# Raw weights of the last layer in an idle buffer, output weights split in the third cosine stage, the logits' maximum by TensorE

## The chip, the cores and the metric

The kernel runs on one core of a Trainium2 chip. The metric is the device time of one execution in microseconds (us); shown is the median of three runs. The profile is of one more execution, whose own time stands beside its span.

## The reference

Sliding-window attention with sinks gives 1536 tokens of 512 features. A mixture of eight experts follows, whose gates are normalised eight times over the rows and columns, and then one wide layer with a cosine.

```python
def _moe_ref(x, w_gate, w1, w2):
    N, D = x.shape                      # 1536, 512
    E = w_gate.shape[1]                 # 8
    logits = x @ w_gate
    logits = logits - logits.max()
    P = np.exp(logits)
    for _ in range(8):
        P /= P.sum(1, keepdims=True) + 1e-09
        P /= P.sum(0, keepdims=True) + 1e-09
        P *= N / E
    out = np.zeros((N, D), dtype=np.float32)
    for e in range(E):
        h = np.maximum(x @ w1[e], 0.0)  # w1[e]: 512 x 1024
        ye = h @ w2[e]                  # w2[e]: 1024 x 512
        out += P[:, e:e + 1] * ye
    return out

def _moe2_ref(x, w_in, w_out):          # 512 x 2048, 2048 x 512
    h = x @ w_in
    g = h * np.cos(h)
    return g @ w_out
```

## The kernel before

The tokens are two batches of 768 (b = 0, 1). After attention there are ten layers: e = 0 to 7 are the experts, with relu; e = 8 and 9 are the two halves of the wide layer, 1024 columns each, with the cosine. A layer does, for each batch in turn, a first product and a second product on TensorE. All operands of products are f32 numbers split into a high and a low f16 half, so that a product is three matmuls for each piece of depth.

The first product (L975 for the experts, in `g1_sums`, L992, for the cosine layers) uses seven products of sums of blocks in place of eight. It needs the x operand `XO[b]` and the first-layer operand `W1O`, both of which hold seven sums of blocks. It is 28 steps long (`GT`, a step is six matmuls of 128x384), the second product (L1043) 24 (`HT_`); a layer is thus 104 steps, and each step ends in `tick()`. The four pairs of cosine layer and batch are called here the first to fourth cosine stage; in them part of the second product is woven into the first as filler. The results of the first product go through five banks: ScalarE copies one (L1014), DVE adds others to it (L1006), and then the cosine runs as ScalarE L900, DVE L903, ScalarE L908 and L909, DVE L912, POOL L914 (high half of `hh`) and L916 (low half). In the expert layers the row is L943, L947, L890, L891, and POOL L892 for the low half.

Side work stands in the program at ticks. `put(t0, every, steps)` puts one step at tick t0 from now, the next `every` ticks later, and each engine runs its instructions in the order in which they were written. A split writes the high half on ScalarE (L190) and at the next tick the low half on DVE (L191).

- Weights of layer e + 1 are prepared in layer e. `w_load` brings the raw f32 ones by SP's queue into a stage buffer of 16 KB per partition (tag "st", one buffer), and finds their scale from the largest element (DVE L168), or, for the output weights of layer 9, from the sum of squares (ScalarE L171, which writes unneeded squares into part of `W2S[1]`). `w1_split` makes sums on POOL (L274 to L277) and splits all into `W1O`; `w2_split` splits eight blocks f = 0 to 7 into `W2S[e % 2]`. The second product of layer 8 reads `W2S[0]`, that of layer 9 `W2S[1]`.
- The x operands of the cosine layers are made from the experts' sum by `x_operand`, six for each batch: three sums into T (L205 to L207), splits of x and T into `xs`, and a transposing DMA on SP (L213) into `XO[b]`. Batch 0's belong to the end of layer 7, batch 1's to layer 8.
- `probabilities` finds the largest logit: DVE reduces each row, and a POOL all-reduce over the partitions gives the maximum, which ScalarE's exponential takes (L660).

The times of the last layer's weights in layer 8 are t2 (its output weights) and t1 (its input weights): tick of the loads, of the first scale step, its spacing, tick of the first split, its spacing.

Of the kernel before, what the change touches and what calls it, by code (L numbers as in the profile page):

```python
# [40 lines left out]
def kernel(  # L41
# [256 lines left out]
    def w2_split(e, st):  # L298
        def sp(f):
            w = W2S[e % 2]  # L300
            split(w[:, 0, f], w[:, 1, f], st["w2"][:, f], wsc[e, "w2"][0])

        return [lambda f=f: sp(f) for f in range(NF)]


    def attention():
# [344 lines left out]
        def probabilities():  # L651
            gm = sm.tile([128, 1], F32, tag="gm", name="gm")
            ga = sm.tile([128, 1], F32, tag="ga", name="ga")
            lf = LG.rearrange("p t e -> p (t e)")
            nc.vector.tensor_reduce(out=gm, in_=lf, axis=AX.X, op=ALU.max)
            nc.gpsimd.partition_all_reduce(ga, gm, 128, MAXOP)

            def rest():
                nc.vector.tensor_scalar(out=ga, in0=ga, scalar1=-1.0, scalar2=None, op0=ALU.mult)
                nc.scalar.activation(out=P.rearrange("p t e -> p (t e)"), in_=lf, func=AF.Exp, bias=ga)  # L660

            return rest

# [146 lines left out]
    def experts(before):  # L810
# [60 lines left out]
        def x2(b):  # L871
# [9 lines left out]
            def ops(c, i):  # L881
                put(2, 1, [x_operand(b, c, i, sx2[b][0])])

# [165 lines left out]
        def layers(e, b, act, so):  # L1049
# [24 lines left out]
            if e == E - 1:  # L1074
                amx, xops = x2(b)

                put(5, 4, [amx[t] for t in tiles])
                put(26, 1, amx[-1:])
                if b:

                    put(HT_ + 5, 7.0, xops[:3])
                    put(HT_ + GT + 9, 4.0, xops[3:])
                else:
                    put(HT_ + 5, 7.0, xops)
            late = None
# [78 lines left out]
        put(T0 + 0, 2, [lambda f=f: gate(f) for f in gates[1]])  # L1164
        put(T0 + 15, 1, [lambda: put(10, 1, [probabilities()])])
        for n, f in enumerate(sinkhorn()):
# [3 lines left out]
        for e in range(E + 2):  # L1170
# [6 lines left out]
            if e + 1 < E + 2:  # L1177

                junk = W2S[1][:, 0, 0:2].rearrange("p f w -> p (f w)").bitcast(BF16) if e == E else None
                ld2, ld1 = w_load(e + 1, "w2", None, st, junk), w_load(e + 1, "w1", None, st)  # L1180

# [6 lines left out]
                if e == E:  # L1188
                    t2, t1 = (0, 6, 5.0, 41, 1.4), (GT + HT_ + -1, GT + HT_ + 5, 3.0, GT + HT_ + GT + 10, 0.5)
                if e == E - 1:  # L1190
# [78 lines left out]
```

## Time and profile before

| what | value |
| --- | --- |
| time, median of 3 runs | 1347.63 us (1346.87 to 1348.05) |
| profiled execution, its own time | 1346.85 us |
| its span from first to last instruction | 1345.1 us |
| mean granted TensorE clock | 0.972 |
| TensorE matmul busy | 1271.7 us, 95% |
| VectorE (DVE) busy | 881.6 us, 66% |
| ScalarE (ACT) busy | 695.7 us, 52% |
| GpSimd (POOL) busy | 654.0 us, 49% |

An engine's share is an average over the whole span; what a step is worth shows only in the stretch where it lies. The line numbers of all rows are those of the kernel before.

### The profile page before, as it was taken

To read this page: it belongs to the slowest core of one execution; us is meant where nothing else is said; L and a number is where in the kernel's file an instruction comes from. 1 tells how busy PE (TensorE), PEld (TensorE's weight loads), DVE (VectorE), ACT (ScalarE), POOL (GpSimd) and SP (SyncE) were. 2 spreads that over 40 slices of the span, in tenths; PEclk is the share of its full clock that TensorE was granted. 3 is DMA by queue.
4 is the path that set the end of the run, shared out by engine and by line. 5 is a ranking of instruction groups with operands and counts; after the bars stand their busy time and mean duration, and the time that the engine had idled before them with its cause. 6 is when DMAs were issued, how large, how long until landed. Compare 5 with 4: busy or idle time off the path is not lost.

```text
span 1345.1 us, 19675 instructions
## 1 busy us (share of the span) xinstructions
PE 1271.7 (95%) x7267; PEld 677.3 (50%) x7267; DVE 881.6 (66%) x1747; ACT 695.7 (52%) x1414; POOL 654.0 (49%) x818
## 2 busy tenths in 40 slices
PE   5657899999999999999999999999999998999998
PEld 4533546454554545455454555545455544445454
DVE  7986734765557655754755585385566778787674
ACT  6665846372644437164453716335372657666452
POOL 5666672540633364173335427234541847377543
PEclk7858999999999999999999999999999998999999
DMA  9999662021113310501321150132112241400001
GB/s 242 178 166 211 138 113 76 2 70 63 57 63 96 108 64 30 174 1 63 102 102 63 32 173 1 63 113 92 63 36 87 44 103 28 104 1 1 32 17 48
DMA packets 138641, 108.25 MB, mean 80 GB/s; under 512 B 98096, under 2 KB 113456, under 8 KB 138544
## 3 DMA queue, kind: packets, MB, share of 16 engines
q1 hardware_dynamic: 124464, 76.69, 22.1%
q0 software_dynamic: 7168, 25.17, 5.9%
q10 hardware_dynamic: 6912, 5.13, 1.5%
q8 instruction: 57, 0.93, 0.3%
q14 instruction: 40, 0.33, 0.1%
HBM read 71.84 MB, written 11.53 MB: 62 GB/s over the span
## 4 chain that ended last, share of the span: by engine, by line
PE 69%; DVE 6%; POOL 4%; ACT 4%; issue 3%; DMA 1%; POOLq 0%; DVEq 0%; ACTq 0%
PE bank L1043 37%; PE bank L975 28%; PE bank L992 4%; DVE tmp L1006 2%; DMA xo<-xs 1%; POOL hh L892 1%; DVE tmp L912 1%; DVE tmp L903 1%; DVE w1o L191 1%; ACT xs L190 1%; DVE xs L191 0%; ACT tmp L908 0%; ACT tmp L900 0%; POOL S L274 0%; POOL S L276 0%
## 5 line engine op out<-in xcount | busy, mean ns | idle before, releaser
L1043 PE MATMUL bank<-w2s,hh 128*128 128x512 f16 x2880 | 637.9, 379 | 5.1 <-POOL hh L916 2.4
L975 PE MATMUL bank<-xo,w1o 128*128 128x384 f16 x2688 | 449.3, 327 | 12.6 <-ACT tmp L943 6.4
L1043 PEld LDWEIGHTS <-hh 128*128 128x128 f16 x2880 | 280.3, 98 | 338.9 <-POOL hh L916 6.3
L892 POOL TENSOR_TENSOR hh<-tmp,hh 128x384 f16<-128x384 f32 x256 | 232.8, 929 | 362.7 <-ACT tmp L891 360.9
L975 PEld LDWEIGHTS <-w1o 128*128 128x128 f16 x2688 | 260.6, 98 | 188.7 <-issue 18.3
L943 ACT ACTIVATE tmp<-bank 128x384 f32<-128x384 f32 x192 | 93.4, 487 | 341.0 <-PE bank L975 340.8
L947 DVE TENSOR_TENSOR tmp<-bank,tmp 128x384 f32<-128x384 f32 x192 | 104.1, 553 | 173.9 <-ACT tmp L943 127.7
L992 PE MATMUL bank<-xo,w1o 128*128 128x384 f16 x672 | 122.1, 333 | 7.3 <-ACT tmp L1014 3.6
L1112 DVE SCALAR_TENSOR_TENSOR acc<-bank,PS,acc 128x512 f32<-128x512 f32 x84 | 62.9, 748 | 82.4 <-PE bank L1043 81.8
L890 ACT ACTIVATE hh<-tmp 128x384 f16<-128x384 f32 x192 | 98.9, 515 | 10.7 <-DVE tmp L947 10.6
L891 ACT ACTIVATE tmp<-tmp 128x384 f32<-128x384 f32 x192 | 100.4, 523 | 6.1
L992 PEld LDWEIGHTS <-w1o 128*128 128x128 f16 x672 | 66.7, 99 | 60.1 <-issue 13.4
L914 POOL TENSOR_SCALAR hh<-tmp 128x384 f16<-128x384 f32 x64 | 45.8, 715 | 85.2 <-DVE tmp L912 72.9
L190 ACT ACTIVATE w1o<-S,s 128x1024 f16<-128x1024 f32 x40 | 45.8, 1145 | 74.5 <-POOL S L277 74.0
L168 DVE TENSOR_REDUCE wm<-st 128x1 f32<-128x1024 f32 x68 | 81.5, 1208 | 0.0
L191 DVE SCALAR_TENSOR_TENSOR w1o<-st,s,w1o 128x512 f16<-128x512 f32 x72 | 65.9, 948 | 13.5 <-ACT w1o L190 13.4
L916 POOL TENSOR_TENSOR hh<-tmp,hh 128x384 f16<-128x384 f32 x64 | 69.4, 1084 | 5.3
L191 DVE SCALAR_TENSOR_TENSOR w1o<-S,s,w1o 128x1024 f16<-128x1024 f32 x40 | 55.0, 1375 | 20.3 <-ACT w1o L190 20.3
L1006 DVE TENSOR_TENSOR tmp<-bank,tmp 128x384 f32<-128x384 f32 x112 | 59.1, 547 | 12.1 <-PE bank L992 8.1
L191 DVE SCALAR_TENSOR_TENSOR w2s<-st,s,w2s 128x512 f16<-128x512 f32 x72 | 56.4, 797 | 9.7 <-ACT w2s L190 9.5
L190 ACT ACTIVATE w2s<-st,s 128x512 f16<-128x512 f32 x72 | 46.6, 708 | 22.8 <-DVE s L160 22.8
L587 POOL TENSOR_TENSOR parts<-xo,parts 128x512 f16<-128x512 f32 (+1 forms) x38 | 42.9, 1128 | 27.3 <-ACT parts L581 16.4
(187 smaller groups left out, 1297.3 us busy)
## 6 DMA issues: line engine op xcount, KB each, us to landing
st<-in_moe_w_dram SPq DMA_DIRECT2D x56, 512.0 KB, 6.2
f<-in_moe_w_in_dram POOLq DMA_DIRECT2D x16, 512.0 KB, 4.4
f<-in_moe_w_out_dram POOLq DMA_DIRECT2D x16, 512.0 KB, 4.2
w2p<-in_moe_w_dram SPq DMA_DIRECT2D x8, 512.0 KB, 4.4
w_in<-x POOLq DMA_DIRECT2D x16, 256.0 KB, 4.8
w_out<-x POOLq DMA_DIRECT2D x16, 256.0 KB, 4.2
st<-w_out SPq DMA_DIRECT2D x8, 512.0 KB, 5.4
st<-w_in SPq DMA_DIRECT2D x8, 512.0 KB, 6.1
```

The lines of the kernel that those rows point to most:

```text
L168: nc.vector.tensor_reduce(out=dst, in_=src, axis=axis, op=ALU.max, apply_absolute_value=True)
L190: nc.scalar.activation(out=hi, in_=src, func=AF.Copy, scale=s)
L191: late.append(lambda: nc.vector.scalar_tensor_tensor(out=lo, in0=src, scalar=s, in1=hi, op0=ALU.mult, op1=ALU.subtract))
L890: nc.scalar.activation(out=hi, in_=src, func=AF.Relu)
L891: nc.scalar.activation(out=dst, in_=src, func=AF.Relu)
L892: nc.gpsimd.tensor_tensor(out=lo, in0=dst, in1=hi, op=ALU.subtract)
L943: nc.scalar.activation(out=t, in_=ps, func=AF.Copy)
L947: nc.vector.tensor_tensor(out=t, in0=ps, in1=t, op=ALU.add)
L975: nc.tensor.matmul(ps, W1O[:, j0 + c, wi, o, kk, :], XO[b][:, kk, o, xi, :], start=(n == 0 and o in (0, 5, 1)), stop=(n == 5), skip_group_ ...
L992: nc.tensor.matmul(ps, W1O[:, j, wi, o, kk, :], XO[b][:, kk, o, xi, :], start=(n == 0), stop=(n == 5))
L1006: nc.vector.tensor_tensor(out=t, in0=x, in1=y, op=ALU.add)
L1043: nc.tensor.matmul(ps, HH[:, hi, f, t * 128:(t + 1) * 128], w[:, wi, f, :], start=(f == order[0] and n == 0), stop=(f == order[-1] and n = ...
```

## The change

The logits' maximum is no longer found by POOL: DVE spreads the row maxima on a diagonal, TensorE multiplies that by ones so that every partition has all of them in a bank, and DVE takes the maximum.

The sums of the x operands are made by DVE for batch 0 and by POOL, as before, for batch 1. Batch 0's operands are put at ticks 57, 62, 67, 72, 77, 82 of layer 7 (they were at 57, 64, 71, 78, 85, 92), batch 1's at 5, 11, 17, 23, 29, 35 of layer 8 (5, 12, 19, 37, 41, 45).

The raw input weights of the last layer are loaded into `W2S[1]`, which is idle in layer 8, seen as f32, at tick 55 (51), and no longer into the stage buffer. The raw output weights stay in the stage buffer until they are split: their squares are at ticks 34, 38, 42, 46 (6, 11, 16, 21), their eight splits at 101, 103, 105, 107, 110, 112, 114, 117 (41 to 50). Layer 9 begins at tick 104. The splits go in the order f = 0, 4, 1, 5, 2, 6, 3, 7.

```diff
--- before.py
+++ after.py
@@ -300,7 +300,8 @@
             w = W2S[e % 2]
             split(w[:, 0, f], w[:, 1, f], st["w2"][:, f], wsc[e, "w2"][0])
 
-        return [lambda f=f: sp(f) for f in range(NF)]
+        fs = [f for j in range(NJ) for f in (j, NJ + j)] if e == w1.shape[0] + 1 else range(NF)
+        return [lambda f=f: sp(f) for f in fs]
 
 
     def attention():
@@ -652,14 +653,21 @@
             gm = sm.tile([128, 1], F32, tag="gm", name="gm")
             ga = sm.tile([128, 1], F32, tag="ga", name="ga")
             lf = LG.rearrange("p t e -> p (t e)")
+            spread = stage.tile([128, 512], F32, tag="x", name="gdiag", bufs=2)[:, 0:128]
             nc.vector.tensor_reduce(out=gm, in_=lf, axis=AX.X, op=ALU.max)
-            nc.gpsimd.partition_all_reduce(ga, gm, 128, MAXOP)
-
-            def rest():
+            nc.vector.tensor_scalar(out=spread, in0=eye, scalar1=gm, scalar2=None, op0=ALU.mult)
+            box = []
+
+            def product():
+                box.append(ring["x"].next()[:, 0:128])
+                nc.tensor.matmul(box[0], ones, spread, start=True, stop=True)
+
+            def read():
+                nc.vector.tensor_reduce(out=ga, in_=box[0], axis=AX.X, op=ALU.max)
                 nc.vector.tensor_scalar(out=ga, in0=ga, scalar1=-1.0, scalar2=None, op0=ALU.mult)
                 nc.scalar.activation(out=P.rearrange("p t e -> p (t e)"), in_=lf, func=AF.Exp, bias=ga)
 
-            return rest
+            return [product, read]
 
 
         at = defaultdict(list)
@@ -879,7 +887,7 @@
                 scales(m1, 1, 1e-30, res, f"x2{b}", lambda *s: sx2.__setitem__(b, s))
 
             def ops(c, i):
-                put(2, 1, [x_operand(b, c, i, sx2[b][0])])
+                put(2, 1, [x_operand(b, c, i, sx2[b][0], g=nc.gpsimd if b else nc.vector)])
 
             return ([lambda t=t: absmax(m[:, t:t + 1], a[:, t, :]) for t in range(NT)] + [scl],
                     [lambda c=c, i=i: ops(c, i) for c in range(2) for i in range(U3)])
@@ -1078,10 +1086,9 @@
                 put(26, 1, amx[-1:])
                 if b:
 
-                    put(HT_ + 5, 7.0, xops[:3])
-                    put(HT_ + GT + 9, 4.0, xops[3:])
+                    put(HT_ + 5, 6.0, xops)
                 else:
-                    put(HT_ + 5, 7.0, xops)
+                    put(HT_ + 5, 5.0, xops)
             late = None
             if e >= E:
                 for t in ps:
@@ -1162,7 +1169,7 @@
         put(6, 1, w1_rest[5:9])
         put(10, 1, w1_rest[9:])
         put(T0 + 0, 2, [lambda f=f: gate(f) for f in gates[1]])
-        put(T0 + 15, 1, [lambda: put(10, 1, [probabilities()])])
+        put(T0 + 15, 1, [lambda: put(3, 3, probabilities())])
         for n, f in enumerate(sinkhorn()):
             put(T0 + 29 + 3 * (n // 3) + (0, 2, 3)[n % 3], 1, [f])
         st = {}
@@ -1177,7 +1184,9 @@
             if e + 1 < E + 2:
 
                 junk = W2S[1][:, 0, 0:2].rearrange("p f w -> p (f w)").bitcast(BF16) if e == E else None
-                ld2, ld1 = w_load(e + 1, "w2", None, st, junk), w_load(e + 1, "w1", None, st)
+                raw = W2S[1].bitcast(F32).rearrange("p a b w -> p (a b) w") if e == E else None
+                raw = raw.rearrange("p (a b) w -> p a (b w)", b=2) if raw is not None else None
+                ld2, ld1 = w_load(e + 1, "w2", None, st, junk), w_load(e + 1, "w1", raw, st)
 
 
                 t2, t1 = (3, 9, 3.0, 28, 2.25), (GT + HT_ + -16, GT + HT_ + 6, 2.5, GT + HT_ + GT + 0, 1.0)
@@ -1186,7 +1195,7 @@
                 if e == 1:
                     t2, t1 = (GT + 1, GT + 9, 2, GT + 20, 1.2), (GT + 31, GT + 46, 2, GT + HT_ + GT + 4, 1.3)
                 if e == E:
-                    t2, t1 = (0, 6, 5.0, 41, 1.4), (GT + HT_ + -1, GT + HT_ + 5, 3.0, GT + HT_ + GT + 10, 0.5)
+                    t2, t1 = (0, 34, 4.0, GT + HT_ + GT + 21, 2.3), (GT + HT_ + 3, GT + HT_ + 9, 3.0, GT + HT_ + GT + 10, 0.5)
                 if e == E - 1:
                     t2, t1 = (3, 8, 2.5, 24, 1.25), (35, 43, 2.0, GT + HT_ + GT + 0, 1.0)
                 put(t2[0], 0, ld2[:4])
```

In the changed kernel the lines after the first hunk are numbered higher: L892 becomes L900, L900 L908, L908 L916, L909 L917, L1014 L1022, L1115 L1122.

On POOL, where the largest logit is found in layer 0 (`gm` and `ga` are its row maxima and the result, S the first-layer weights' sums), there stood:

```order
L185 TENSOR_TENSOR xs<-T,xs 128x4x128
L892 TENSOR_TENSOR hh<-tmp,hh 128x384 x8
L656 ISA
L656 ISA ga<-gm 128x1
L892 ISA
L892 TENSOR_TENSOR hh<-tmp,hh 128x384 x8
L274 TENSOR_TENSOR S<-st 128x256
```

and now stand:

```order
L207 TENSOR_TENSOR T<-acc_75,T 128x128
L185 TENSOR_TENSOR xs<-T,xs 128x4x128
L900 TENSOR_TENSOR hh<-tmp,hh 128x384 x16
L274 TENSOR_TENSOR S<-st 128x256
L275 TENSOR_TENSOR S<-S,st 128x256
```

The all-reduce and two instructions without operands beside it are gone, and the sixteen subtractions follow one another.

On ScalarE, near the end of the first cosine stage (L171 is a sum of squares of the raw output weights, L190 a split for an x operand, L1014 the copy of a bank), there stood:

```order
L908 ACTIVATE tmp<-tmp,scl 128x384
L909 ACTIVATE tmp<-tmp 128x384
L900 ACTIVATE tmp<-tmp,scl 128x384
L171 ACTIVATE w2s_73,wm<-st 128x1024
L190 ACTIVATE xs<-T,s 128x4x128
L908 ACTIVATE tmp<-tmp,scl 128x384
L909 ACTIVATE tmp<-tmp 128x384
L1014 ACTIVATE tmp<-bank_84 128x384
```

and now stand:

```order
L917 ACTIVATE tmp<-tmp 128x384
L908 ACTIVATE tmp<-tmp,scl 128x384
L190 ACTIVATE xs<-T,s 128x4x128
L908 ACTIVATE tmp<-tmp,scl 128x384
L916 ACTIVATE tmp<-tmp,scl 128x384
L917 ACTIVATE tmp<-tmp 128x384
L908 ACTIVATE tmp<-tmp,scl 128x384
L916 ACTIVATE tmp<-tmp,scl 128x384
L917 ACTIVATE tmp<-tmp 128x384
L1022 ACTIVATE tmp<-bank_84 128x384
L916 ACTIVATE tmp<-tmp,scl 128x384
L917 ACTIVATE tmp<-tmp 128x384
```

The square ahead of the copy is gone from there, and the split of an x operand stands two cosines ahead of the copy.

On ScalarE, as the third cosine stage begins (L1115 and L1122 write the second stage's last results, L190 into w1o is the last first-layer split), there stood:

```order
L190 ACTIVATE w1o<-S,s 128x1024
L1115 ACTIVATE acc_75<-bank_85,scl 128x512
L1115 ACTIVATE acc_75<-bank_82,scl 128x512
L1014 ACTIVATE tmp<-bank_79 128x384
L900 ACTIVATE tmp<-tmp,scl 128x384
L908 ACTIVATE tmp<-tmp,scl 128x384
```

and now stand:

```order
L190 ACTIVATE w1o<-S,s 128x1024
L1122 ACTIVATE acc_75<-bank_85,scl 128x512
L190 ACTIVATE w2s_73<-st,s 128x512 x2
L1122 ACTIVATE acc_75<-bank_82,scl 128x512
L1022 ACTIVATE tmp<-bank_79 128x384
L190 ACTIVATE w2s_73<-st,s 128x512
L908 ACTIVATE tmp<-tmp,scl 128x384
L190 ACTIVATE w2s_73<-st,s 128x512
L916 ACTIVATE tmp<-tmp,scl 128x384
L917 ACTIVATE tmp<-tmp 128x384
L908 ACTIVATE tmp<-tmp,scl 128x384 x2
L190 ACTIVATE w2s_73<-st,s 128x512
```

Two splits of the output weights have come ahead of the copy and three more among the first cosines.

## Rows read from the trace of the kernel before

**Rows 1.** The page: the span, busy time by engine, TensorE in 40 slices.

```profile
span 1345.1 us, 19675 instructions
...
PE 1271.7 (95%) x7267; PEld 677.3 (50%) x7267; DVE 881.6 (66%) x1747; ACT 695.7 (52%) x1414; POOL 654.0 (49%) x818
...
PE   5657899999999999999999999999999998999998
```

**Rows 2.** Windows: stretch, length, busy time by engine, granted clock, DMA share, GB/s.

```profile
1088.72:1136.89 48.17, 41.28 (x210) 21.44 (x209) 38.74 (x86) 32.83 (x62) 28.18 (x33) 0.89 0.33 82
1160.09:1197.69 37.60, 35.44 (x206) 19.93 (x205) 32.18 (x64) 22.32 (x42) 17.65 (x22) 1.00 0.20 64
1222.86:1259.06 36.20, 35.41 (x206) 19.86 (x205) 32.87 (x59) 25.18 (x48) 23.72 (x25) 1.00 0.00 1
1282.46:1317.54 35.08, 35.08 (x206) 19.95 (x205) 30.25 (x58) 22.98 (x44) 21.32 (x24) 1.00 0.02 9
1132.00:1134.00 2.00, 2.00 (x8) 0.99 (x7) 2.00 (x5) 1.17 (x3) 1.92 (x3) 0.50 1.01 189
```

**Rows 3.** Chain of waits, TensorE, 1000 to 1346 us: total, times, longest us.

```profile
PE bank L992 <- ACT tmp L1014: 3.6, 2, 3.2
PE bank L992 <- DMA xo<-xs: 3.3, 2, 2.1
```

**Rows 4.** Timeline of TensorE: start, length, instructions, idle before in brackets.

```profile
1091.43 6.23 PE L992 MATMUL bank<-xo,w1o 128*128 128x384 f16 x27 [2.06 <-DMA xo<-xs]
...
1131.09 4.00 PE L992 MATMUL bank<-xo,w1o 128*128 128x384 f16 x12 [3.19 <-ACT tmp L1014]
...
1161.98 10.40 PE L992 MATMUL bank<-xo,w1o 128*128 128x384 f16 x63 [1.25 <-DMA xo<-xs]
...
1228.34 6.01 PE L992 MATMUL bank<-xo,w1o 128*128 128x384 f16 x36 [0.44 <-ACT tmp L1014]
```

**Rows 5.** Timeline of POOL around the all-reduce.

```profile
229.41 0.38 POOL L656 PARTITION_ALL_REDUCE ga<-gm  x1 [5.92 <-DVE tmp L947]
...
236.79 5.27 POOL L892 TENSOR_TENSOR hh<-tmp,hh 128x384 f16<-128x384 f32 x6 [7.01 <-ACT tmp L891]
```

**Rows 6.** Groups by line and shape: count, busy us, mean ns, idle before.

```profile
L1043 PE MATMUL bank<-w2s,hh 128*128 128x512 f16 x2880 | 637.9, 379 | 5.1 <-POOL hh L916 2.4 <-POOL hh L892 2.0 <-POOL hh L914 0.4
...
L191 DVE SCALAR_TENSOR_TENSOR w2s<-st,s,w2s 128x512 f16<-128x512 f32 x72 | 56.4, 797 | 9.7 <-ACT w2s L190 9.5
...
L190 ACT ACTIVATE w2s<-st,s 128x512 f16<-128x512 f32 x72 | 46.6, 708 | 22.8 <-DVE s L160 22.8
...
L205 POOL TENSOR_TENSOR T<-acc 128x256 f32<-128x256 f32 x18 | 15.1, 839 | 11.6 <-DVE acc L1112 6.9 <-DVE xs L191 4.2
...
L206 DVE TENSOR_TENSOR hh<-acc,hh 128x128 f32<-128x128 f32 x3 | 2.7, 903 | 0.1
...
L778 PE MATMUL bank<-cs,ones 128*128 128x8 f32 x16 | 2.4, 225 | 0.5 <-DVE cs L773 0.5
```

**Rows 7.** Timeline of ScalarE in the first cosine stage.

```profile
1127.85 1.04 ACT L171 ACTIVATE w2s<-st 128x1024 bf16<-128x1024 f32 x1
...
1128.89 0.70 ACT L190 ACTIVATE xs<-T,s 128x512 f16<-128x512 f32 x1
...
1130.56 0.47 ACT L1014 ACTIVATE tmp<-bank 128x384 f32<-128x384 f32 x1
```

**Rows 8.** Timeline as the third cosine stage begins.

```profile
1227.81 0.49 ACT L1014 ACTIVATE tmp<-bank 128x384 f32<-128x384 f32 x1
...
1233.77 1.31 POOL L916 TENSOR_TENSOR hh<-tmp,hh 128x384 f16<-128x384 f32 x1
```

**Rows 9.** Timeline of POOL sums and DVE splits.

```profile
1210.93 0.73 POOL L276 TENSOR_TENSOR S<-st 128x256 f32<-128x256 f32 x1
...
1213.56 1.35 DVE L191 SCALAR_TENSOR_TENSOR w1o<-S,s,w1o 128x1024 f16<-128x1024 f32 x1 [3.97 <-ACT w1o L190]
...
1213.79 1.71 POOL L276 TENSOR_TENSOR S<-st 128x256 f32<-128x256 f32 x1
```

## The prediction

> **What bounds the kernel now.** The first lines of the page come first: TensorE is busy 1271.7 of 1345.1 us [rows 1], so the time is TensorE's own work plus some 73 us in which it is idle. Almost all of those lie in the attention part before 250 us, which the change does not touch, and there is little else to win: 2.0 us of waits of the second product for POOL's low half of hh from L892 [rows 6], and what the four cosine stages lose. So I read those four next, one stretch for each first product [rows 2]. They hold nearly the same matmuls (210, 206, 206, 206) and take 48.17, 37.60, 36.20 and 35.08 us. The fourth has no idle TensorE (35.08 busy of 35.08): it is the yardstick. The losses are 13.1, 2.5 and 1.1 us.
>
> Then the chain of waits in that part [rows 3]: TensorE waits 3.6 us for ScalarE's copy of a first product's bank, 3.3 us for the transposed x operand; five waits for the cosines' low half of hh from L916 make 2.4 [rows 6]. The timeline puts places to them [rows 4]: 2.06 us at 1089 us and 1.25 us at 1161 us, where the first and the second stage begin and their last transpose has not landed; 3.19 us at 1128 us inside the first stage; 0.44 us at 1228 us as the third begins. The two long ones in the first stage cost more than themselves, for the clock falls behind them: 27 matmuls took 6.23 us and 12 took 4.00 us, where 36 took 6.01 us (0.167 each) in the third stage; at 0.167 they would be 4.50 and 2.00. The granted clock is 0.50 at 1132 to 1134 us [rows 2], its 1.2 GHz level, after the engine stood idle. So the first costs 2.06 + 1.73 = 3.8 us, the second 3.19 + 2.00 = 5.2 us.
>
> **The change part by part.** The sum is made against the profiled execution, 1346.85 us, which is 0.78 below the median of 1347.63.
>
> (a) *The logits' maximum.* The all-reduce itself is 0.38 us of POOL, but it stands behind 5.92 us of idle POOL, and the next subtraction behind 7.01 us [rows 5]. The latter is put down to ScalarE, but in the order an instruction without operands stands ahead of each of the two, so I read both gaps as POOL changing its program, there and back. The second product then waits the 2.0 us for hh [rows 6]. The order shows the eight and eight subtractions become sixteen in a row. New are one DVE multiply, one f32 product on TensorE, one DVE maximum. No 128x128 f32 product is in the trace; from below, the f32 product of 8 columns takes 0.225 us [rows 6]; from above, 16 of those, 3.6 us, if it went by columns. A matmul of 384 columns in f16 takes 0.167, so I take 0.3. The product waits for nothing then, as it is put three ticks after its input. −2.0 + 0.3 = **−1.7** (−1.8 to +1.6).
>
> (b) *The start of the first cosine stage.* The six x operands of batch 0 are put at ticks 57, 62, ... 82 of the last expert layer instead of 57, 64, ... 92. The last stands 10 ticks earlier; a tick of a first product is six matmuls of 0.167, 1.0 us, so about 10 us against a wait of 2.06. Their sums move from POOL to DVE, 18 instructions. From the rows: the first sum took POOL 0.84 us and the second of a triple took DVE 0.90 us in the attention part [rows 6]; so about 1.5 us of DVE for each operand, 9 us over some 35, on an engine at 66% [rows 1]. DVE would have to fall 8 us behind for the operand to be late again. **−3.8** (−3.8 to 0).
>
> (c) *Inside the first cosine stage.* The order of ScalarE shows it. Before, a sum of squares stands ahead of the copy that TensorE waits for: 1.04 us, then 0.70 us of an x operand, and the copy only at 1130.56 [rows 7]. The squares go to tick 34 and later, into the second product, where ScalarE has little to do. But the fourth x operand of batch 1 is now in this stage as well (ticks 5, 11, 17, 23 and then 29, 35; before three). Each costs ScalarE three splits, DVE three and POOL three sums. So four squares of 1.04 us go, 4.2 us of ScalarE, and one operand comes, about 1.2 us (its largest split 0.70, the others half and a quarter of its elements). Of the 5.2 us of the long stall I take nine tenths, **−4.7**. Bounds: all that the stage loses beyond (b), 13.1 − 3.8 less 0.7 for its four more matmuls, −8.6; or a stall of the same size at another operand, 0.
>
> (d) *The start of the second stage.* The last operand of batch 1 is put at tick 35 instead of 45, and with it its transpose on SP's queue. Nothing else is put ahead of it there. **−1.25** (−1.25 to 0).
>
> (e) *The third stage pays.* The second-layer weights of the last layer stay raw in their stage buffer until then, as the second-layer buffer holds the first-layer raws. So eight splits, each one ScalarE and one DVE instruction, move from the second product of the first stage into the end of the second stage and the start of the third: ticks 101, 103, then 105 to 117. By the rows ScalarE takes 0.708 and DVE 0.797 us for each [rows 6], 5.7 and 6.4 us in all. The order shows two ahead of the first copy L1014, which before ended at 1228.3 and let TensorE go on after 0.44 us, and four more woven into the first cosines. Each delays the chain from that copy to hh's first low half (1233.77) [rows 8]. The split of block 1 also must wait for the last DVE split of first-layer weights that reads the same buffer. I walk it as +1.25 us at the copy and about +3 us at hh, of which some overlaps: **+4**. Bounds: two splits on the path, +1.3; all eight on DVE and the bank wait once more, +7.
>
> One more price is in the rows: a POOL sum took 0.73 us alone and 1.71 us while a DVE split ran beside it [rows 9], 0.98 longer. Eight more splits can so hold POOL for 7.8 us in a stage where POOL makes every hh; I have 0 of it in the +4, since DVE is late before POOL is, and all of it in rival 1. The Trainium skill has a rule for this (SBUF — State Buffer, section Terms): DVE and GpSimd share one port pair, an instruction holds it to its end, and the loser blocks fully. By that rule each split can cost POOL its whole 0.797 us, 6.4 us for the eight; the trace's 0.98 agrees with a block and not with sharing.
>
> (f) *The sums on DVE in the last expert layer, the raw load into the idle buffer 4 ticks later.* TensorE has no wait there now worth a row; POOL is relieved of 1.8 us per operand, DVE loaded with 1.5. **0** (−0.6 to +0.6). If the cover failed, relu's sums on DVE would be late and with them hh.
>
> Sum: −1.7 − 3.8 − 4.7 − 1.25 + 4 = −7.45, so 1339.4 by the profiled execution; with the 0.78 by which it lies below the median, 1340.2. I say **1340.0 us**.
>
> **The rivals.** *1, slower: the third stage starves.* All eight splits go ahead of the cosines on ScalarE and DVE one after the other: 5.7 + 6.4 = 12.1 us on the path, and behind a stall over 3 us the clock falls as at 1128 us, +2.0. For each of the eight DVE splits POOL is held as well (0.98 each), which keeps hh late when DVE has caught up. Then −11.45 + 14.1 = +2.7: 1350.3 us. It decides when more than 11.5 us fall on the path. For it: POOL's, DVE's and ScalarE's work is tightest here, DVE 32.87 of 36.20 us [rows 2], so 6.4 us more is more than the stretch holds, and POOL's blocking comes on top. Against: the ring of five banks and the second product's work that fills in lets later products run, and two of the eight are ahead of the stage. Chance 0.10.
>
> *2, the first stage is not relieved:* the fourth operand puts a new stall where the square stood, DVE being the bound (38.74 of 48.17 us busy [rows 2], the most of the four). Then (c) is 0: −1.7 − 3.8 − 1.25 + 4 = −2.75, 1344.9 us. Chance 0.20.
>
> *3, all goes well:* (c) at −8 and (e) at +1.3: −15.4, 1332.2 us. Chance 0.10.
>
> *4, the moved transposes change nothing:* operands queue behind DVE, (b) and (d) are 0, the rest as summed: −2.4, 1345.2 us; within 0.2%. Chance 0.07.
>
> **How the numbers follow.** My forecast has 0.53. Measurement of this kernel tells about 0.2%, 2.7 us, from no change. The forecast's own range, with (c) between −7 and −3 and (e) between +2 and +6, is 1336 to 1344. To leave out no more than 2 in 10, I reach to rival 2 and 4 above (1346) and towards rival 3 below (1333). Faster by over 0.2% (below 1344.9): the forecast, rival 3, half of 2 and a little of 4: 0.53 + 0.10 + 0.12 + 0.03 = 0.78. Within 0.2%: the rest of 2 and 4, and a little of 1: 0.13. Slower: 0.09.
>
> **What would show it.** (a) No gap on POOL around 223 to 237 us, and TensorE without the two hh waits at 237 and 241. (b), (d) The waits for the transposed operand of 2.06 and 1.25 us gone, and the granted clock 1.00 at the first stage's start. (c) No wait over 1 us for L1014's copy in the first stage, its stretch 38 to 42 us. (e) The third stage's stretch 39 to 42 us instead of 36.2, with DVE splits into w2s between the reductions, and new waits for hh's low half or the copy. Wrong it would be if the third stage took over 46 us, if the first kept over 45, or if a new stall came in the last expert layer, where DVE has the sums.

## The result, and the profile after

The changed kernel is slower: 1356.36 us (median of 5 runs, 1353.58 to 1358.04) against 1347.53 (median of 5), a ratio of 1.0066 with a 95% interval of 1.0051 to 1.0081, about 9 us. The forecast was 1340.0 with a range up to 1346.

The page of the changed kernel, span, busy time and TensorE in 40 slices, beside [rows 1]:

```profile
span 1354.2 us, 19686 instructions
...
PE 1272.6 (94%) x7269; PEld 677.6 (50%) x7269; DVE 891.0 (66%) x1767; ACT 695.3 (51%) x1414; POOL 641.4 (47%) x799
...
PE   5657899999999999999999999999999996998998
```

TensorE's work is nearly the same; the seventh slice from the right, with the first cosine stage's second product in it, falls from 8 to 6. To see where time came and went, the span is cut at places that both programs have: start of layer 0's second batch, start of layer 1, start of the first cosine stage, end of its first product, start of the second, third and fourth stage. Windows of the changed kernel, columns as in [rows 2]:

```profile
203.96:266.67 62.71, 62.30 (x421) 34.53 (x419) 39.81 (x105) 30.92 (x61) 25.69 (x32) 1.00 0.10 36
266.67:1086.85 820.18, 818.83 (x4388) 428.48 (x4386) 516.00 (x854) 389.34 (x785) 349.75 (x403) 1.00 0.23 75
1086.85:1126.64 39.79, 36.18 (x207) 19.74 (x205) 34.02 (x71) 27.33 (x53) 22.52 (x27) 1.00 0.23 53
1126.64:1163.31 36.67, 28.00 (x110) 11.07 (x109) 16.87 (x35) 17.17 (x32) 15.76 (x20) 0.86 0.37 95
1163.31:1225.14 61.83, 59.33 (x315) 30.37 (x314) 49.47 (x85) 37.46 (x67) 41.01 (x47) 1.00 0.00 1
1225.14:1291.59 66.45, 60.36 (x314) 29.90 (x313) 48.53 (x82) 35.67 (x66) 30.37 (x34) 1.00 0.06 20
1291.59:1354.20 62.61, 58.54 (x313) 30.41 (x311) 39.77 (x72) 27.58 (x52) 28.45 (x32) 1.00 0.08 30
```

And the windows of the kernel before that [rows 2] does not hold. The stretch of 48.17 us there is not cut like the one above: TensorE ends the first product at 1134.88, and the stretch runs on to 1136.89, over three matmuls of the second product and the small product of a scale. Cut alike, the first product takes 46.16 us and the second 25.21:

```profile
203.46:269.05 65.59, 62.76 (x419) 33.83 (x418) 39.69 (x103) 30.93 (x61) 26.53 (x33) 1.00 0.10 34
269.05:1088.72 819.67, 818.82 (x4387) 428.19 (x4386) 506.57 (x833) 389.53 (x785) 358.02 (x419) 1.00 0.23 73
1088.72:1134.88 46.16, 39.74 (x207) 20.93 (x206) 36.94 (x78) 31.54 (x60) 26.41 (x31) 0.90 0.34 86
1134.88:1160.09 25.21, 24.38 (x111) 10.61 (x110) 19.96 (x40) 17.88 (x33) 13.90 (x20) 0.97 0.23 45
1160.09:1222.86 62.77, 59.27 (x314) 30.26 (x313) 49.32 (x86) 37.47 (x67) 41.01 (x47) 1.00 0.12 38
1222.86:1282.46 59.60, 58.81 (x313) 30.33 (x312) 42.45 (x74) 30.79 (x58) 31.77 (x34) 1.00 0.06 23
```

The difference, stretch by stretch: layer 0's second batch 65.59 to 62.71 (−2.9); the expert layers 819.67 to 820.18 (+0.5); first product of the first stage 46.16 to 39.79 (−6.4); its second product 25.21 to 36.67 (**+11.5**); the second stage 62.77 to 61.83 (−0.9); the third 59.60 to 66.45 (**+6.9**); the rest 0. With 0.5 us by which layer 0 began later in this execution, that is +9.1, the difference of the spans, 1354.2 and 1345.1.

The chain of waits of TensorE, 1000 to 1356 us (total, times, longest), where [rows 3] had 3.6 for the copy and 3.3 for the transposed operand:

```profile
PE bank L1000 <- ACT tmp L1022: 6.1, 6, 1.7
PE bank L1051 <- ACT acc L1122: 5.1, 1, 5.1
PE bank L1051 <- POOL hh L924: 4.9, 10, 0.8
PE bank L1051 <- POOL hh L922: 2.5, 2, 2.3
```

The waits for the transposed operand are gone. New is one of 5.1 us for ScalarE's L1122, which empties a bank of the second product. The timeline of TensorE around it:

```profile
1124.69 2.11 PE L1000 MATMUL bank<-xo,w1o 128*128 128x384 f16 x12 [1.55 <-ACT tmp L1022]
...
1133.04 0.81 PE L1051 MATMUL bank<-w2s,hh 128*128 128x512 f16 x2 [2.35 <-POOL hh L922]
...
1145.26 18.21 PE L1051 MATMUL bank<-w2s,hh 128*128 128x512 f16 x72 [5.12 <-ACT acc L1122]
```

The stall ahead of the copy at the end of the first product is 1.55 us now, and the 12 matmuls behind it take 2.11, not 4.00 [rows 4]. But two waits of 2.35 and 5.12 follow in the second product, and 72 matmuls then take 18.21 us, as the clock falls (granted 0.86 over the stretch); in the first run below the same 72 take 15.70, so 2.5 us of this are the clock's. Followed back, L1122 stands on ScalarE behind a split of the sixth x operand, which waits 4.43 us for its sums T:

```profile
1138.69 0.79 ACT L190 ACTIVATE xs<-acc,s 128x256 f16<-128x256 f32 x2
1143.91 0.72 ACT L190 ACTIVATE xs<-T,s 128x512 f16<-128x512 f32 x1 [4.43 <-POOL T L207]
1144.54 0.67 ACT L1122 ACTIVATE acc<-bank,scl 128x512 f32<-128x512 f32 x1
```

and the sums stand on POOL behind the last cosines' high and low halves (L922, L924), which POOL does without a gap:

```profile
1139.27 1.22 POOL L924 TENSOR_TENSOR hh<-tmp,hh 128x384 f16<-128x384 f32 x1
1140.46 0.68 POOL L922 TENSOR_SCALAR hh<-tmp 128x384 f16<-128x384 f32 x1
1141.22 0.91 POOL L924 TENSOR_TENSOR hh<-tmp,hh 128x384 f16<-128x384 f32 x1
1142.09 0.72 POOL L205 TENSOR_TENSOR T<-acc 128x256 f32<-128x256 f32 x1
1142.89 0.45 POOL L206 TENSOR_TENSOR T<-acc,T 128x128 f32<-128x128 f32 x1
1143.42 0.45 POOL L207 TENSOR_TENSOR T<-acc,T 128x128 f32<-128x128 f32 x1
```

The last low half is done at 1142.13 us, 15.5 us after TensorE ended the first product (11.4 in the kernel before, 1146.31 for 1134.88): the cosine work left over by the first product, with the operands among it, is that long, and what is written among it or after it waits. In the kernel before, the split of T of the fourth operand waits for its sums too, but two copies L1115 stand ahead of it on ScalarE, and TensorE goes on:

```profile
1143.45 1.33 ACT L1115 ACTIVATE acc<-bank,scl 128x512 f32<-128x512 f32 x2
1148.09 0.72 ACT L190 ACTIVATE xs<-T,s 128x512 f16<-128x512 f32 x1 [3.30 <-POOL T L207]
```

### The profile page after: what moved, and what is told of

Same layout as the page of the kernel before. It is cut to its first block, busy times and chain, and to the rows that moved or that the text cites. A ratio compares the mean times of both kernels' runs of the same rounds, so it can differ in the third digit from the quotient of the medians.

```text
span 1354.2 us, 19686 instructions
## 1 busy us (share of the span) xinstructions
PE 1272.6 (94%) x7269; PEld 677.6 (50%) x7269; DVE 891.0 (66%) x1767; ACT 695.3 (51%) x1414; POOL 641.4 (47%) x799
## 4 chain that ended last, share of the span: by engine, by line
PE 72%; DVE 6%; ACT 4%; POOL 3%; issue 2%; DMA 0%; POOLq 0%; ACTq 0%
PE bank L1051 41%; PE bank L983 29%; PE bank L1000 3%; DVE tmp L1014 2%; DVE tmp L920 1%; DVE tmp L911 1%; ACT tmp L916 1%; POOL hh L924 1%; POOL hh L922 1%; DVE w2s L191 1%; ACT w2s L190 1%; ACT tmp L917 1%; ACT tmp L908 1%; DVE xs L191 0%; POOL S L276 0%
## 5 line engine op out<-in xcount | busy, mean ns | idle before, releaser
L900 POOL TENSOR_TENSOR hh<-tmp,hh 128x384 f16<-128x384 f32 x256 | 233.8, 932 | 375.2 <-ACT tmp L899 373.0
L899 ACT ACTIVATE tmp<-tmp 128x384 f32<-128x384 f32 x192 | 100.4, 523 | 6.1
L922 POOL TENSOR_SCALAR hh<-tmp 128x384 f16<-128x384 f32 x64 | 45.0, 703 | 105.9 <-DVE tmp L920 105.9
L190 ACT ACTIVATE w1o<-S,s 128x1024 f16<-128x1024 f32 x40 | 45.8, 1145 | 76.3 <-POOL S L277 75.8
L168 DVE TENSOR_REDUCE wm<-st 128x1 f32<-128x1024 f32 x64 | 76.7, 1208 | 0.0
L924 POOL TENSOR_TENSOR hh<-tmp,hh 128x384 f16<-128x384 f32 x64 | 67.7, 1057 | 5.3
L191 DVE SCALAR_TENSOR_TENSOR w1o<-st,s,w1o 128x512 f16<-128x512 f32 x64 | 56.9, 921 | 14.0 <-ACT w1o L190 14.0
L1014 DVE TENSOR_TENSOR tmp<-bank,tmp 128x384 f32<-128x384 f32 x112 | 59.4, 547 | 9.5 <-ACT tmp L1022 5.3
L190 ACT ACTIVATE w2s<-st,s 128x512 f16<-128x512 f32 x72 | 47.0, 707 | 22.8 <-DVE s L160 22.8
```

The costliest lines, as they stand in the source:

```text
L190: nc.scalar.activation(out=hi, in_=src, func=AF.Copy, scale=s)
L191: late.append(lambda: nc.vector.scalar_tensor_tensor(out=lo, in0=src, scalar=s, in1=hi, op0=ALU.mult, op1=ALU.subtract))
L899: nc.scalar.activation(out=dst, in_=src, func=AF.Relu)
L900: nc.gpsimd.tensor_tensor(out=lo, in0=dst, in1=hi, op=ALU.subtract)
L924: nc.gpsimd.tensor_tensor(out=lo, in0=k, in1=hi, op=ALU.subtract)
L1014: nc.vector.tensor_tensor(out=t, in0=x, in1=y, op=ALU.add)
```

## The experiments

All times are medians beside runs of the kernel before on the same chip; the interval is that of the ratio to it. Line numbers in their profiles are those of the changed kernel, shifted by 1 where a line was added. Diffs are against the changed kernel unless another is named. The expectations count the runs in the order in which they were made: first batch 1's operands at their old ticks, second squares back, third sums on DVE, fourth the maximum and batch 0's operands, fifth splits spread, sixth the last two operands back, seventh squares between the operands, and so on.

**Batch 1's operands at their old ticks.**

```diff
-                    put(HT_ + 5, 6.0, xops)
+                    put(HT_ + 5, 7.0, xops[:3])
+                    put(HT_ + GT + 9, 4.0, xops[3:])
```

> The changed kernel, but batch 1's x operands at the ticks of before (5, 12, 19, then 37, 41, 45 of layer 8). Theory A (POOL): the second product of the first cosine stage takes 36.7 us instead of 23.2 because the sums of operands 4 to 6 stand among the cosines' last high and low halves on POOL, so that hh and the split of T are late; then it falls back to 24 to 26 us, the second stage's start waits some 1.3 us again, and the whole is 1344 to 1347 us. Theory B (squares): the squares of the output weights at ticks 34 to 46 on ScalarE hold up the copy that frees TensorE's bank; then nothing is won, 1355 to 1358 us. Theory C (third stage): the eight splits are the loss and the second product's length is only a shift; then also about 1356 us.

1347.5 us, ratio 0.9994 (0.9984 to 1.0004): some 9 us of the changed kernel's time come from these ticks. Windows of the first stage's first and second product and of the third stage:

```profile
1089.32:1128.42 39.10, 35.94 (x206) 19.71 (x205) 32.62 (x71) 26.70 (x51) 23.08 (x26) 1.00 0.22 50
1128.42:1154.73 26.31, 23.99 (x110) 10.30 (x108) 16.02 (x35) 17.65 (x34) 16.21 (x22) 1.00 0.32 60
1216.70:1283.15 66.45, 60.36 (x313) 29.86 (x312) 48.54 (x82) 35.66 (x66) 30.37 (x34) 1.00 0.06 20
```

The second product falls from 36.67 to 26.31, just above what theory A said, and the first is hardly shorter (39.10 for 39.79). Theory A's place is right, and the wait for the copy that frees a bank is 0.27 us. The 1.3 us at the second stage's start did not return: the waits for the operand that [rows 4] showed there are away although the operands are as late as before (the reason stands under (d) below). And the third stage is as long as in the changed kernel, 66.45.

**Squares back in the first product.**

```diff
-                    t2, t1 = (0, 34, 4.0, GT + HT_ + GT + 21, 2.3), ...
+                    t2, t1 = (0, 6, 5.0, GT + HT_ + GT + 21, 2.3), ...
```

> The changed kernel, but the squares of the output weights at ticks 6, 11, 16, 21 of layer 8, as before the change. Theory A (POOL): the second product of the first stage stays above 33 us and the first product, which has squares and four operands now, grows by 2 to 5 us: 1356 to 1361 us. Theory B (squares): the second product falls to 24 to 27 us, 1346 to 1350 us.

1358.5 us, 1.0080 (1.0065 to 1.0095). Cut at the end of the first product as above, the first takes 42.72 and the second 36.17 us, and the wait of 5.12 us for L1122 stands unchanged with no square left near it. Theory B falls, and what theory A said comes out (2.9 us more in the first product).

**Batch 1's sums on DVE.**

```diff
-put(2, 1, [x_operand(b, c, i, sx2[b][0], g=nc.gpsimd if b else nc.vector)])
+put(2, 1, [x_operand(b, c, i, sx2[b][0], g=nc.vector)])
```

> The changed kernel, but the x operand sums of batch 1 on DVE as well. Theory A (POOL): POOL loses six times 1.8 us in the first stage, the wait of 5.1 us behind the split of T goes, and the second product takes 26 to 31 us: 1348 to 1352 us in all, unless DVE, 34 of 39.8 us busy in the first product, takes over as the limit. Theory B (squares): the second product stays above 33 us: 1355 us or more.

1357.8 us, 1.0076 (1.0059 to 1.0093): a miss for theory A as it was put, since POOL has none of the sums now and the second product still takes 32.98 us (the first has grown to 43.83). The split of T waits on ScalarE all the same, for DVE:

```profile
1145.73 0.72 ACT L190 ACTIVATE xs<-T,s 128x512 f16<-128x512 f32 x1 [2.45 <-DVE T L207]
```

and TensorE waits 4.19 us for L1122 behind it. Thus it isn't POOL's load alone: it is the place in the order. Both engines tried have the cosines' work of the stage ahead of the sums, and ScalarE stops at the split with the banks' copies behind it.

**Only the last two operands back.**

```diff
-                    put(HT_ + 5, 6.0, xops)
+                    put(HT_ + 5, 6.0, xops[:4])
+                    put(HT_ + GT + 13, 4.0, xops[4:])
```

> The changed kernel, but only the last two of batch 1's six x operands are put back, to ticks 41 and 45; the fourth stays at tick 23 of the first stage's first product. Theory A2 (the drain): the loss is made by operands 5 and 6, whose sums stand behind the last cosines' work and hold ScalarE in front of the copies that free the banks; then the second product takes 25 to 28 us instead of 36.7 and the whole 1346 to 1349 us. Theory F (the fourth operand overloads the first product): then a backlog stays, the second product takes 31 us or more and the whole 1351 to 1356 us.

1349.3 us, 1.0006 (0.9994 to 1.0019). The first stage's two products:

```profile
1087.63:1127.42 39.79, 36.18 (x206) 19.74 (x205) 34.03 (x71) 27.32 (x53) 22.52 (x27) 1.00 0.23 51
1127.42:1156.73 29.31, 26.60 (x111) 11.04 (x108) 14.50 (x35) 17.25 (x32) 15.04 (x20) 0.88 0.34 72
```

The fifth and sixth operand make 7.4 us of the second product (36.67 to 29.31), the fourth 3.0 (29.31 to 26.31). The wait of 5.12 us is gone; the one of 2.35 for hh stands, and is 0.89 when the fourth operand is put back too. The fourth costs the first product 0.7 and is paid in the second too, between the two theories.

**The maximum and batch 0's operands alone.** Against the kernel before, beside the new `probabilities`:

```diff
-put(2, 1, [x_operand(b, c, i, sx2[b][0])])
+put(2, 1, [x_operand(b, c, i, sx2[b][0], g=nc.gpsimd if b else nc.vector)])
...
-                    put(HT_ + 5, 7.0, xops)
+                    put(HT_ + 5, 5.0, xops)
```

> Of the change only the maximum by TensorE and batch 0's operands (sums on DVE, ticks 57 to 82); everything of layer 8's weights and of batch 1's operands as before the change. By the step sizes read from the two traces, 1.9 us at the maximum and 3.8 at the start of the first stage, about 5.7 us less than before: 1341 to 1343 us. If the earlier start of the first stage only moves its waits to a later place (the stall of 3.2 us for the bank's copy, the second stage's start), 1344 to 1347 us.

1343.5 us, 0.9969 (0.9955 to 0.9982): faster, and between the two expectations. The first stage's two products:

```profile
1087.99:1130.55 42.56, 37.96 (x207) 20.36 (x205) 34.66 (x74) 31.55 (x60) 24.44 (x28) 0.94 0.22 49
1130.55:1155.76 25.21, 24.35 (x110) 10.63 (x109) 19.97 (x40) 17.89 (x33) 13.90 (x20) 0.97 0.23 45
```

Its first product is 3.6 us shorter than before, the second as before, and the stall of 3.19 us with the slow 12 matmuls stands.

**The maximum alone.** Against the kernel before:

```diff
-            nc.gpsimd.partition_all_reduce(ga, gm, 128, MAXOP)
+            nc.vector.tensor_scalar(out=spread, in0=eye, scalar1=gm, scalar2=None, op0=ALU.mult)
+                nc.tensor.matmul(box[0], ones, spread, start=True, stop=True)
+                nc.vector.tensor_reduce(out=ga, in_=box[0], axis=AX.X, op=ALU.max)
...
-        put(T0 + 15, 1, [lambda: put(10, 1, [probabilities()])])
+        put(T0 + 15, 1, [lambda: put(3, 3, probabilities())])
```

> The kernel before with the maximum by TensorE as its only change. In the profiles with it, the stretch from the start of layer 0's second batch to the start of layer 1 is 62.7 us, and 65.6 before: 2.9 us less, not the 1.7 that the prediction summed. If that is the step's whole effect, the time is 2 to 4 us below the kernel before, 1343.5 to 1345.5, and the first cosine stage still begins with a wait of about 2 us for the transposed operand. If the saving is taken back later, by operands that come late all the same, it is within 1 us of before.

1345.6 us, 0.9985 (0.9975 to 0.9994), some 2 us less. The first stage begins with the wait still, 1.68 us, but this time the clock did not fall behind it: 27 matmuls in 4.55 us, not 6.23 [rows 4].

```profile
1092.53 4.55 PE L1000 MATMUL bank<-xo,w1o 128*128 128x384 f16 x27 [1.68 <-DMA xo<-xs]
```

**Splits spread wider in the third stage** (against the first run of this study).

```diff
-GT + HT_ + GT + 21, 2.3)
+GT + HT_ + GT + 21, 3.6)
```

> As the first run of this study (batch 1's operands at their ticks of before), and the eight splits of the output weights spread wider: from tick 101 every 3.6 instead of every 2.3, so that the last is at 126. That run took 1347.5 us and its third stage 41.5 us for the first product, 5.3 more than before. Theory D (burst): the loss comes from the splits that stand ahead of the first cosines; spread out, the stretch falls to 37 to 39 us and the whole to 1343 to 1345 us. Theory E (load): DVE is 37.4 of 41.5 us busy and 6.4 of it are the splits; as seven or eight of them still fall into the same 28 steps, the stretch stays at 40 to 42 and the whole at 1346.5 to 1348.5 us.

1345.4 us, 0.9984 (0.9972 to 0.9997). Between the theories: the third stage's first product falls from 41.5 to 38.85 us, but its second grows, with a new wait of 0.98 us for hh, and the stage as a whole goes from 66.45 to 64.83, still 5.2 above before.

**The low halves left out; the high halves left out** (both against the first run). POOL writes zeros where DVE's, or ScalarE's, eight instructions stood.

```diff
-            split(w[:, 0, f], w[:, 1, f], st["w2"][:, f], wsc[e, "w2"][0])
+            nc.scalar.activation(out=w[:, 0, f], ..., func=AF.Copy, scale=...)
+            late.append(lambda: nc.gpsimd.memset(w[:, 1, f], 0.0))
```

> As the first run (1347.5 us), with the low halves of the last layer's output weights left out: POOL, half idle in the third stage, writes zeros where DVE's eight splits stood. Theory E (DVE's load): the third stage, 66.4 us from its start to the fourth's against 59.6 before the change, falls to 60 to 62 us and the whole to 1341 to 1343.5. Theory G (ScalarE's eight splits in front of copies and cosines): it stays at 64 us or more, the whole at 1345.5 to 1347.5.

> As the first run (1347.5 us), with the high halves of the last layer's output weights left out: POOL writes zeros where ScalarE's eight splits stood, DVE's eight stay. Theory E (DVE's load): the third stage stays at 64 us or more, the whole at 1345.5 to 1347.5. Theory G (ScalarE): it falls to 60 to 62 us, the whole to 1341 to 1343.5.

1340.2 us, 0.9944 (0.9923 to 0.9966), and 1346.7 us, 0.9997 (0.9987 to 1.0006). The third stage from its start to the fourth's, without the low halves and without the high ones:

```profile
1218.04:1278.51 60.47, 58.72 (x313) 30.45 (x312) 41.00 (x74) 35.42 (x66) 35.05 (x42) 1.00 0.06 22
```

```profile
1215.68:1281.37 65.69, 60.66 (x313) 29.91 (x312) 48.13 (x82) 31.02 (x58) 35.19 (x42) 1.00 0.06 21
```

Without DVE's eight it is 60.47, 6.0 less and within 0.9 of before; without ScalarE's eight 65.69, 0.8 less. DVE's own time in the stage, 6.4 us by [rows 6], is about the price; theory E is borne out. Without DVE's eight splits POOL could no longer be held by them either, so these two runs alone do not part the two; the trace of the changed kernel does. POOL's 34 instructions of the third stage take 30.37 us there and 31.77 before, so they were not lengthened on the whole, and its first high half of the stage begins when DVE's L920 is done. The rule that the prediction set beside this part (DVE and GpSimd share one port pair and the loser blocks; the Trainium skill, SBUF — State Buffer, section Terms) thus shows no price of its own in this stage. POOL's first high half:

```profile
1238.49 0.74 POOL L922 TENSOR_SCALAR hh<-tmp 128x384 f16<-128x384 f32 x1 [10.63 <-DVE tmp L920]
```

**All splits ahead of the third stage** (against the first run).

```diff
-t2, t1 = (0, 34, 4.0, GT + HT_ + GT + 21, 2.3), (GT + HT_ + 3, GT + HT_ + 9, 3.0, GT + HT_ + GT + 10, 0.5)
+t2, t1 = (0, 34, 4.0, GT + HT_ + GT + 16, 1.1), (GT + HT_ + 3, GT + HT_ + 9, 2.0, GT + HT_ + GT + 3, 0.5)
```

> As the first run (1347.5 us), with both sets of splits earlier: the input weights' from tick 83 instead of 90, the output weights' from tick 96 every 1.1 instead of 101 every 2.3, all eight before the third stage begins. If the third stage's loss is the splits inside it, its first product falls from 41.5 to 36 to 38 us and the whole to 1341 to 1344 us. If the input weights' sums on POOL (22.3 of 25.1 us busy in the second stage's second product) set when a split can begin, the splits only pile up ahead of the third stage's first copy, and the whole stays at 1346 to 1350 us.

1356.3 us, 1.0065 (1.0046 to 1.0084), worse than either theory, though each is right in part. With no split of either kind left in it, the third stage takes 58.39 us from its start to the fourth's and TensorE is never idle in it, so its loss is the splits inside it. The price has moved one product ahead: in the second stage's second product TensorE waits once, for 15.89 us:

```profile
1216.57 17.25 PE L1051 MATMUL bank<-w2s,hh 128*128 128x512 f16 x72 [15.89 <-ACT acc L1123]
```

It is of the same kind as in the first stage, and larger. On ScalarE the splits of S stand ahead of the first L1123 copy, each waiting for POOL's sums:

```profile
1204.10 1.15 ACT L190 ACTIVATE w1o<-S,s 128x1024 f16<-128x1024 f32 x1 [4.48 <-POOL S L277]
...
1214.18 1.15 ACT L190 ACTIVATE w1o<-S,s 128x1024 f16<-128x1024 f32 x1 [2.12 <-POOL S L277]
...
1215.85 0.67 ACT L1123 ACTIVATE acc<-bank,scl 128x512 f32<-128x512 f32 x1
```

Those are splits of the input weights, which went earlier too; the eight of the output weights all stand behind that copy, from 1224.08 on.

**A version without the raw load: squares between the operands** (against the run with the maximum and batch 0's operands).

```diff
-t2, t1 = (0, 6, 5.0, 41, 1.4), (GT + HT_ + -1, GT + HT_ + 5, 3.0, GT + HT_ + GT + 10, 0.5)
+t2, t1 = (0, 11, 7.0, 46, 0.9), (GT + HT_ + 3, GT + HT_ + 9, 3.0, GT + HT_ + GT + 10, 0.5)
```

> As the fourth run (maximum by TensorE and batch 0's operands alone, 1343.5 us), with the squares at ticks 11, 18, 25, 32 between the operands (5, 12, 19) instead of 6, 11, 16, 21, the eight splits from tick 46 every 0.9 (41 every 1.4) and the input weights' load at tick 55. If the stall of 3.2 us at the bank's copy is a square standing directly ahead of it together with an operand's split, it falls below 1.5 us, no stretch at half the clock follows, and the whole takes 1339 to 1341.5 us. If the first stage is short of ScalarE and DVE time as a whole, or the splits, now nearer the second stage, hold its start, 1343 to 1346 us.

1342.4 us, 0.9958 (0.9941 to 0.9974), the fastest complete kernel here. The first product takes 40.80 us (42.56 in the run that it builds on), the second 24.70 (25.21). The stall is 2.15 us, not below 1.5, and 12 matmuls near half the clock follow all the same. It is as long with no square in the whole first product (first run), so a square makes about 1 us of the 3.19.

**Operands denser on top of that.**

```diff
-                    put(HT_ + 5, 7.0, xops[:3])
+                    put(HT_ + 5, 5.0, xops[:3])
-t2, t1 = (0, 11, 7.0, 46, 0.9), ...
+t2, t1 = (0, 17, 5.0, 46, 0.9), ...
```

> As the seventh run (squares apart, 1342.4 us), with batch 1's first three operands at ticks 5, 10, 15 instead of 5, 12, 19, and the squares at 17, 22, 27, 32. The stall of 2.15 us for the bank's copy at 1126 us stands in the runs with and without squares in the first product, always behind the third operand. If that operand makes it, it moves or falls below 1 us when the operand is earlier, where the ring still has free banks, and the whole takes 1338.5 to 1341 us. If the cosine chain alone makes it, it stays where it is, 1341.5 to 1343.5 us; if the denser operands overload the start of the stage, 1344 us or more.

1344.5 us, 0.9982 (0.9973 to 0.9992). The stall falls to 0.75 us, as the first theory has it, but this does not show that the third operand makes it. Waits of 1.53 and 0.79 us for hh come earlier in the first product, and TensorE reaches the stall 3.2 us later after the stage's start (38.2 for 35.0); the copy itself comes 1.8 us later, not earlier. What makes the 2.15 us stays open. The first product is as long as it was, 40.92 us, and the second grows to 27.56: the denser operands overload the stage, as the last of the three expectations has it.

## Why the prediction was wrong

Point by point, by its own letters.

(a) Right in kind, too small: −1.7 forecast, −2.9 in the stretch, 62.71 for 65.59. TensorE has 62.30 us of work there and 0.41 idle, 2.83 before, so more idle pieces went than the two waits of 2.0. The f32 product took 0.2 us, near the 0.3. One sign was wrong: the gap on POOL does not go, but ends 6 us sooner (the next subtraction at 230.90 for 236.79 [rows 5]). POOL idles 6.92 us there without any all-reduce, until ScalarE's L899 is done, so of the two gaps that the prediction read as POOL changing its program the first is mere waiting for work; only what followed the all-reduce was its price, and what POOL did in it no row shows. Alone the step gives 2 us.

(b) Right: −3.8 forecast, −3.6 measured (46.16 to 42.56 with the maximum and batch 0's operands alone). The clock's part of it, 1.73 us, is no fixed price, as the run with the maximum alone shows.

(c) Right in kind, too large: −4.7 forecast, −2.8 measured (42.56 to 39.79). Moving the squares out gave 3.5 (39.10 in the first run), and the fourth operand cost 0.7. By the stretch of [rows 2] the first product would be 8.4 us shorter, close to the −8.5 of (b) and (c) together; but 2.01 us of that are the four matmuls at the end of that stretch, which only stand elsewhere now and which the prediction took at 0.7. That agreement comes from where the stretch was cut, and would be luck.

(d) −1.25 forecast, −0.9 measured, but as a saving it is empty. The wait at the second stage's start is also away with the operands at their old ticks. There the last transpose leaves no earlier than before, 22.84 us after the end of the first product (1151.26 and 1128.42) for 23.02 (1157.90 and 1134.88); what changed is that TensorE comes later, as the second product takes 26.31 us for 25.21. In the changed kernel it leaves some 4 us earlier, but TensorE comes 11.5 us later.

**The step that failed** is in (c) and (d): "into the second product, where ScalarE has little to do", and "Nothing else is put ahead of it there". The moved operands were charged to the first product alone, and the second product had no term. The runs show +11.5 us there. The three operands that were put 10 to 14 ticks earlier are 10.4 of it (36.67 to 26.31; some 9 us of the whole time); the rest of the change makes the other 1.1, and the squares alone no more than 0.5 (36.67 with them, 36.17 without). TensorE is 11.4 us ahead of the cosines at the end of the first product before the change, and 15.5 after it. An operand at ticks 23 to 35 is written into the queues among them, so that the engine that makes its sums reaches them late, and ScalarE, which must split them, cannot get to the copies that free the second product's banks. Before, at ticks 37 to 45, the sums stood behind the cosines as well, but the split that waits for them stood behind the first two of those copies. It is this wait, and not ScalarE's load, that the prediction left out: ScalarE is busy only 17.17 of the 36.67 us. No run here put the late splits behind the copies with the sums at their new ticks.

(e) Right in kind, mis-sized: +4 forecast, +6.9 measured, at the upper bound of +7. That bound was all eight DVE splits on the path, 6.4 us. They are, nearly: without them the stage is 6.0 shorter; ScalarE's eight cost 0.8. The wait at the copy is 1.66 us for 0.44, as the +1.25 had it, and the first product, 41.48 us, is where the sign put it (39 to 42); DVE's part was too small, and 1.6 of the 6.9 fall again into a second product (23.40 to 24.97) that had no term. The order in which DVE does them, ahead of and between the reductions that free the banks:

```profile
1230.28 0.75 DVE L191 SCALAR_TENSOR_TENSOR w2s<-st,s,w2s 128x512 f16<-128x512 f32 x1
1231.55 0.74 DVE L191 SCALAR_TENSOR_TENSOR w2s<-st,s,w2s 128x512 f16<-128x512 f32 x1
1232.21 0.55 DVE L1014 TENSOR_TENSOR tmp<-bank,tmp 128x384 f32<-128x384 f32 x1
1232.68 0.74 DVE L191 SCALAR_TENSOR_TENSOR w2s<-st,s,w2s 128x512 f16<-128x512 f32 x1
1233.34 1.02 DVE L1014 TENSOR_TENSOR tmp<-bank,tmp 128x384 f32<-128x384 f32 x2
1235.18 0.75 DVE L191 SCALAR_TENSOR_TENSOR w2s<-st,s,w2s 128x512 f16<-128x512 f32 x1 [0.83 <-ACT w2s L190]
```

The price of POOL, 0.73 to 1.71 us, was rightly left out of the sum.

(f) 0 forecast, +0.5 measured: DVE took 9.4 us more in the expert layers (506.57 to 516.00), as the 9 us said, and nearly all of it is hidden.

Rival 1 had the sign, but the wrong stage and reason; its own place, the third stage, gave 6.9 and not 14.1. No rival named the second product of the first stage. By terms: −2.9 − 6.4 − 0.9 + 6.9 + 0.5 would be −2.8; the term without a place, 11.5, turns it to +8.7.

Three slips of the prediction touch neither the forecast nor its failure. Rival 3's terms add up to −13.45, so 1334.2 us, and not to −15.4; half of rival 2 is 0.10 and not 0.12; and of TensorE's 73 us of idle time some 16 lie behind the start of layer 1 at 269 us, so that not almost all lie before 250.

## What to carry to other kernels

When work is moved earlier in an in-order program, price it in the stage where its queue drains, and not only where it is written: look how far TensorE runs ahead of the other engines there, and which instruction behind the moved one frees TensorE's next buffer. An instruction that waits for another engine's late result is dear when it stands ahead of such a copy: 5.1 us here, 15.9 in one of the runs. A stretch whose busiest helper is at 33 of 36 us has no room for 6 us more: spread wider, they still cost 5.2 of 6.9 us, and with both sets of splits put ahead of the stage, the stage before it was held up for 15.9. And before two stretches are compared, see that both are cut at the same instruction.

## What was not expected of the hardware

The same stall had two prices. In two runs TensorE waited 2.14 and 2.15 us for the same copy; the 12 matmuls behind it took 2.11 us in the first run and 3.79 in the one with squares apart, about the two levels of the clock:

```profile
1126.48 2.11 PE L1000 MATMUL bank<-xo,w1o 128*128 128x384 f16 x12 [2.14 <-ACT tmp L1022]
```

```profile
1126.55 3.79 PE L1000 MATMUL bank<-xo,w1o 128*128 128x384 f16 x12 [2.15 <-ACT tmp L1022]
```

Likewise 12 matmuls behind a wait of 1.55 us took 2.11 us in the changed kernel and 4.00 in the run with batch 1's sums on DVE. What decides between them these runs do not show, so a term for the clock after a stall needs both ends.

The profiled executions begin layer 0's second batch between 203.5 and 207.8 us with the same program ahead of it. A span alone thus says little below 4 us, while the stretches between two such places, where the program is the same, repeat within 0.2 us.
